# Threshold attention with a feed-forward block: three small moves in the hand-written order of the work

## The chip, the cores and the metric

The kernel runs on one core of a Trainium2 chip. The core has five engines that work side by side: TensorE (PE; its weight loads are shown as PEld), VectorE (DVE), ScalarE (ACT), GpSimd (POOL) and SyncE (SP), which here mostly issues DMA transfers. Each engine takes its instructions strictly in the order in which the program lists them, and waits where an instruction needs something from another engine or from a transfer. The metric is the time of one execution in microseconds (us), less is better. Before the change it is 1319.89 us, the median of three runs (1319.29 to 1322.22).

## What is computed

Eight batches, eight heads, 576 tokens, head width 64; everything is float32, apart from the two weight matrices, which arrive as float64.

```python
scores = scale * np.matmul(q, k.transpose(0, 1, 3, 2))
thresh = np.max(scores, axis=-1, keepdims=True) - tau
scores = np.where(scores >= thresh, scores, -1000000000.0)
scores = scores - np.max(scores, axis=-1, keepdims=True)
attn = np.exp(scores)
attn = attn / (np.sum(attn, axis=-1, keepdims=True) + 1e-09)
attn_out = np.matmul(attn, v)
...
mu = np.mean(x, axis=-1, keepdims=True)          # x: attn_out, heads side by side, width 512
var = np.mean((x - mu) ** 2, axis=-1, keepdims=True)
xn = (x - mu) / np.sqrt(var + 1e-06) * g_ln
ch = np.maximum(xn @ w_ch1, 0.0) @ w_ch2          # 512 -> 2048 -> 512
out = x + ch
```

## The kernel before, in words

**Slots.** The attention is cut into 72 slots, nine for each batch (`SLOTS`). In a slot TensorE makes four 128x576 blocks of scores (`scores`, L434), in two PSUM tiles of two blocks each. VectorE takes the negated maxima of each tile (L450, two reductions), ScalarE exponentials (L463, four), VectorE multiplies them by the mask of the threshold and sums (L473, four), GpSimd divides (L490). VectorE then transposes the blocks in 32x32 pieces (L559), SP writes them to a scratch tensor in DRAM (`scr`, L580) and reads them back in another arrangement (`em`, L594, and `er`, L599); TensorE multiplies them by the values (L638, and L649 for the last 64 tokens) near the end of the next slot, and ScalarE copies the result to x (L663). The scratch write and the read back therefore have most of a slot (some 17 us) for themselves.

**Loads of q and k.** A unit is a pair of heads; its q and k lie in one buffer each (`q_in`, `k_in`). `turn` (VectorE, L368 to L378, after GpSimd's scaling of q at L350) transposes them into the operands of the scores; only then may `load_qk` (eight DMA issues, L120) fetch the next unit's. From slot 11 on, the loads that belong to the first three slots of a batch are put off to the place called "behind", which is after the scratch write of that slot (18 loads in all). The load in a batch's last slot stands right behind `turn`, ahead of the scratch write.

**Groups.** The feed-forward part works on 16 groups of 288 tokens (`g`), two for each batch, and its matmuls are dealt out between those of the slots. When the x of a group is complete, `group_ready` lays out: the mean over features as a matmul (L710, spread by ScalarE, L718), the difference x minus mean (`centre`, L744: four operations of 128x288 on VectorE, one for each block of features, into `xc`), the squares (L1463, ScalarE; added by GpSimd, L1032), and `sum_x` (L946): three differences of blocks of `xc` on VectorE and a fourth on GpSimd, which the matmuls "chain" and "sc<-t" read. `xc` feeds the first matmuls directly. For even groups centring and the three differences stand ahead of the slot's maxima in VectorE's order, with one addition (L1224) of the group before behind them; for odd groups they end just before the next slot. `sum_early` draws such additions forward.

**PSUM for the feed-forward matmuls** is one pool of two banks (`ps_ff`). A new product must wait until ScalarE has copied the one before the last out of its bank: the copies `last`, `part` and `y` (L1199), of a chain (L978), of a hidden tile (L1071).

**Weights.** float64 is turned into float32 on the chip, in 32 pieces (`Weights`): two ScalarE operations (L277, L282), three on VectorE (`begin`, L292 to L299), one or two on GpSimd (`carry`, L307 and L310). This happens within the first eleven slots. A table `BEGUN` says how many pieces each part of a slot begins; `carry_all` then issues GpSimd's part of all pieces that were begun, newest first. In the slots from the sixth on it stands behind the maxima, GpSimd's thresholds (L454) and the first two exponentials. The raw pieces are fetched by SP into whatever buffer is free (`stage`, `x_room`, `y_room` and others).

**Sums of weights.** `sums_of_w1` (L910: three small operations on VectorE and one on GpSimd each time) is advanced at every twelfth step of the second half of groups 1 and 2.

The order on each engine is the order of the calls in the main loop (L1513 on); `at_quarter` puts a call at a place of a slot ("-3", 0, "behind" and so on), and `run` issues what was put there.

Of the kernel before, what the change touches and what calls it, by code (L numbers as in the profile page):

```python
# [12 lines left out]
ALU = mybir.AluOpType  # L13
# [5 lines left out]
def kernel(  # L19
# [37 lines left out]
    NK = DM // 128  # L57
# [3 lines left out]
    TOK = S // 2  # L61
    QH = 256
    SLOTS = 2 * HP + 1
# [31 lines left out]
    units = [(b, hp) for b in range(B) for hp in range(HP)]  # L95
# [33 lines left out]
    def load_v(u):  # L129
# [21 lines left out]
        out=tau_sb, in_=bass.AP(tensor=tau.tensor, offset=tau.offset, ap=[[0, 128], [1, 1]])  # L151
# [5 lines left out]
    for t in v_rest:  # L157
# [9 lines left out]
        out=scl_sb, in0=tau_sb, scalar1=0.0, scalar2=SCALE, op0=ALU.is_ge, op1=ALU.mult  # L167
    )
    nc.vector.tensor_scalar(
        out=low_sb, in0=tau_sb, scalar1=0.0, scalar2=BIG, op0=ALU.is_lt, op1=ALU.mult  # L170
    )
    nc.vector.scalar_tensor_tensor(
        out=low_sb, in0=tau_sb, scalar=-1.0, in1=low_sb, op0=ALU.mult, op1=ALU.subtract
# [5 lines left out]
    class Weights:  # L179
# [141 lines left out]
        def carry_all(self):  # L321

            self.prepare_to(0, False)
            for i in reversed(range(self.carried, self.begun)):
                self.carry(i)
            self.carried = self.begun

# [19 lines left out]
    def scale_q(u, q_in):  # L347

        for at in (slice(0, 8), slice(8, NB)) if u == 0 else (slice(0, NB),):
            nc.gpsimd.tensor_scalar(  # L350
                out=q_in[:, at], in0=q_in[:, at], scalar1=scl_sb, scalar2=1.0,
                op0=ALU.mult, op1=ALU.mult,
            )
# [251 lines left out]
    groups, sums = {}, {}  # L605
# [129 lines left out]
    def centre(g):  # L735
        nonlocal issued
        while waiting_mean:
            issued += next(queue[0])[1]
        xc = centred[g] = ffn.tile([128, NK, TOK], F32, tag="xc", bufs=1, name="xc")
        mean = means.pop(g)  # L740
        while any(d[4] in EARLY for d in drops):
            drops.pop(0)[-1]()
        for c in range(NK):
            nc.vector.tensor_tensor(  # L744
                out=xc[:, c], in0=groups[g][:, c], in1=mean, op=ALU.subtract
            )


# [607 lines left out]
    def ffn_steps(g):  # L1356
        if g in carried:
            yield from carried.pop(g)
        rb = yield from (first_part if g < 2 else first_units)(g)
        sums = sums_of_w1({1: (0, 1), 2: (2,)}.get(g, ()))  # L1360
        for i, step in enumerate((second_quarters if g else second_plain)(g, rb)):
            if i % 12 == 11:
                next(sums, None)
            yield step

# [19 lines left out]
    def at_quarter(n, i, fn, *args):  # L1385
        later_calls.setdefault((n, i), []).append((fn, args))

    def run(n, i):
        for fn, args in later_calls.pop((n, i), ()):
            fn(*args)  # L1390
# [58 lines left out]
    def group_ready(g):  # L1449
        first = divmod(ready(g), QUARTERS)  # L1450
        before = divmod(ready(g) - 1, QUARTERS) if g else first
        if g == 1:
            at_quarter(*before, lambda: among.append(g))
        else:
            at_quarter(*before, mean_of, g)
            at_quarter(*(first if g and first[1] else before), centre, g)
            if g > 1:
                sq = squares_of(g)
                at_quarter(*before, sum_x, g, (0, 1, 2))
                at_quarter(first[0], -3, sum_early, *(("12",) if g == 2 else EARLY))  # L1460
                at_quarter(
                    first[0], -3,
                    lambda: nc.scalar.activation(sq, centred[g], func=AF.Square),  # L1463
                )
                at_quarter(first[0], -1, add_squares, sq, 1, 2)
                at_quarter(first[0], 1, add_squares, sq, 3)
                at_quarter(first[0], 1, sum_x, g, (3,))
        at_quarter(*first, lambda: queue.append(ffn_steps(g)))
# [44 lines left out]
    for n in range(NS):  # L1513
        b, s = divmod(n, SLOTS)
        masks_at, behind_at, end_at = BEGUN[min(n, len(BEGUN) - 1)]
        run(n, -3)
        if n == 1:
            constants(26)
        scores(b, s)
        run(n, -2)  # L1520
        run(n, -1)
        if n + 1 < HP:
            scale_q(n + 1, loaded[n + 1][0])
        rest = exponentials(n)
        es, thr = next(rest)
        conversion.carry_all()
        run(n, 0)
        if n == HP + 2:
            next(rest, None)
        if n >= HP:  # L1530
            conversion.fetch(1 if n == FIRST + 2 else 3, -1 if n > FIRST else 1)
        run_first(stores)
        if early_at(n):
            convert(masks_at)
        second_part(n, 0)
        while drops and drops[0][0] is nc.gpsimd:
            drops.pop(0)[-1]()
        next(rest, None)

        run(n, "load")  # L1540
        if n >= SLOTS - 2 and (n + 2) % SLOTS < HP and n < NS - 2:
            at_quarter(n, "behind", load_v, (n + 2) // SLOTS * HP + (n + 2) % SLOTS)
        u = (n + 1) // SLOTS * HP + (n + 1) % SLOTS
        if (n + 1) % SLOTS < HP and u < len(units):
            turn(u)
            if n > SLOTS + 1 and n % SLOTS < SLOTS - 1 and u + 1 < len(units):
                at_quarter(n, "behind", load_qk, u + 1)
            elif u + 1 < len(units) and u != 2:
                load_qk(u + 1 if u > 1 else 3)
        if n < HP:  # L1550
            conversion.fetch(2 if n else 1)
        if n < SLOTS + HP:
            run_all(aside)
        if not early_at(n):
            convert(masks_at)
        if n < FIRST:
            conversion.prepare_to(end_at)
        elif n == FIRST:
            conversion.prepare_to(behind_at, False)
        run(n, 1)  # L1560
        second_part(n, 1)
        if n > FIRST:
            conversion.prepare_to(behind_at, False)
        blocks_go = by_blocks(n)
        diags = weights(n, es, thr, blocks_go)
        run_all(aside)
        drip()
        if n < SLOTS:
            run_all(stores)
        conversion.begin_to(behind_at)  # L1570
        run(n, 2)
        second_part(n, 2)
        if n < FIRST:
            conversion.carry_all()
        box = []
        if blocks_go:
            conversion.fetch(0 if n == FIRST + 2 else 3, wait=0)
            conversion.prepare_to(end_at, False)
            scr = turn_blocks(b, s, es)
            for fn, args in reversed(later_calls.pop((n, "behind"), ())):  # L1580
                fn(*args)
            run_all(sums_due)
            if n == FIRST:
                conversion.take(e_room[1])
            if n == FIRST:
                conversion.fetch(3)
            conversion.carry_all()
            at_quarter(n + 1, 0, lambda b=b, s=s, scr=scr, box=box: box.append(fetch(b, s, scr)))
        else:

            made = turn_weights(s, es, diags)
            for i, at in enumerate(
                (-1, -1, 0, 0)
            ):
                if i == 3 and n + 1 == FIRST:
                    at_quarter(n + 1, 0, conversion.prepare_to, BEGUN[n + 1][0], False)
                if i < 3:
                    at_quarter(n + 1, at, next, made)
                else:
                    at_quarter(n + 1, at, lambda made=made, box=box: box.append(next(made)))  # L1600
        at_quarter(
            n + 1, 1 if b == 0 and s <= HP else 3,
            lambda b=b, s=s, box=box: values_of(b, s, box[0]),
        )
        if s in (HP, 2 * HP):
            group_ready(2 * b + (s > HP))
        if not plain_at(n):
            run_all(aside)
        drip({nc.vector: 4, nc.gpsimd: 6})
        if HP <= n < FIRST:  # L1610
            conversion.fetch(5)
        run(n, 3)
        if b == 0 and s < HP - 1:
            load_v(s + 1)
        if n < FIRST:
            conversion.prepare_to(BEGUN[n + 1][0] - (n == FIRST - 1))
        second_part(n, 3)
        conversion.begin_to(end_at)
        if n < FIRST:
            conversion.carry_all()  # L1620
        conversion.prepare_to(0, False)
        if FIRST <= n < SLOTS:
            conversion.prepare_to(BEGUN[n + 1][0], False)
        if not plain_at(n):
            run_all(aside)
        drip({nc.vector: 2, nc.gpsimd: 0})
# [40 lines left out]
```

## Time and profile before

| | before |
|---|---|
| median of 3 runs | 1319.89 us |
| the profiled execution | 1319.15 us |
| its span, first to last instruction | 1317.3 us |
| mean granted TensorE clock | 0.995 |
| busy: PE, PEld | 1272.3, 1081.5 us |
| busy: DVE, POOL, ACT | 953.4, 677.1, 528.1 us |

The profile is of one execution. A row of the timeline reads: start in us, duration in us, engine, line of the kernel, operation, output<-input and its shape, how many instructions were merged into the row, and in brackets the idle time of the engine before it with what ended it. A row of the view of waits reads: who, at which line, waited for whom; total in us, how often, the longest. TensorE's fp32 matmul appears as two records, so "x16" is four calls of `product`. Durations of merged rows run from the start of the first to the end of the last. Busy times overlap between engines, so they don't add up to the span.

### The profile page before, as it was taken

The numbers are of one execution on the slowest core, as the hardware profiler recorded it, in microseconds if no ns is written. First come the engines' busy times: TensorE is split into PE (matmuls) and PEld (weight loads), VectorE is DVE, ScalarE is ACT, GpSimd is POOL, SyncE is SP. The second block draws the span as 40 slices with busy tenths as digits, with TensorE's granted clock in tenths as the row PEclk, the third lists the DMA queues.
The fourth block names the chain that finished last, engine by engine and source line by source line (L and its number), as shares of the span: only waits on it lengthen the run. The fifth ranks groups of instructions, "written<-read, shape, count | busy, mean of one in ns | idle before, by whom it ended". The sixth has DMA issues, their size and how long they took to land.

```text
span 1317.3 us, 44852 instructions
## 1 busy us (share of the span) xinstructions
PE 1272.3 (97%) x19272; PEld 1081.5 (82%) x19272; DVE 953.4 (72%) x1760; ACT 528.1 (40%) x1189; POOL 677.1 (51%) x888
## 2 busy tenths in 40 slices
PE   8999889999999999999999999999999999999997
PEld 6765556878888898988989898988989889888987
DVE  7879877987778767677867777787676768777122
ACT  5866242242433424343343434334343423434231
POOL 3465565544537364545636454364645456364324
PEclk9999899999999999999999999999999999999999
DMA  8947856565655767466665667547675666554211
GB/s 165 267 130 184 202 161 180 188 186 159 187 188 175 212 158 209 154 196 182 163 196 191 192 166 183 196 155 211 168 208 173 195 170 167 175 187 167 52 44 20
DMA packets 337478, 226.01 MB, mean 172 GB/s; under 512 B 247616, under 2 KB 292928, under 8 KB 329216
## 3 DMA queue, kind: packets, MB, share of 16 engines
q1 hardware_dynamic: 331168, 222.26, 58.3%
q8 instruction: 151, 2.47, 0.8%
q10 hardware_dynamic: 5952, 0.74, 0.4%
q0 software_dynamic: 160, 0.15, 0.1%
q14 instruction: 47, 0.39, 0.1%
HBM read 134.22 MB, written 88.87 MB: 169 GB/s over the span
## 4 chain that ended last, share of the span: by engine, by line
PE 64%; DVE 6%; DMA 4%; POOL 2%; SPq 1%; issue 1%; ACT 1%; POOLq 0%; DVEq 0%; ACTq 0%
PE seg L103 22%; PE chain L103 11%; PE p L103 9%; PE sc L434 7%; PE sc L638 7%; PE sc L103 6%; DVE e L473 2%; DMA er<-scr 2%; PE sc L649 2%; DVE neg L450 1%; DMA scr<-e 1%; SPq L120 1%; DVE e L559 1%; ACT e L463 1%; POOL sum L692 1%
## 5 line engine op out<-in xcount | busy, mean ns | idle before, releaser
L450 DVE TENSOR_REDUCE neg<-sc 128x2 f32<-128x1152 f32 x144 | 188.9, 1353 | 176.4 <-PE sc L434 174.9
L490 POOL TENSOR_SCALAR e<-e,den 128x576 f32<-128x576 f32 x264 | 205.5, 791 | 111.5 <-DVE den L478 111.3
L103 PE MATMUL seg<-hidden,w 128*64 128x144 f32 x3840 | 249.7, 288 | 2.6 <-DVE hidden L1183 2.6
L103 PE MATMUL p<-xc,w 128*64 128x288 f32 (+1 forms) x2128 | 240.3, 371 | 8.9 <-ACT last L1199 7.4
L103 PEld LDWEIGHTS seg<-hidden,w 128*64 128x64 f32 x3840 | 236.4, 138 | 13.2 <-issue 12.3
L473 DVE SCALAR_TENSOR_TENSOR e<-sc,thr,e 128x576 f32<-128x576 f32 x288 | 222.4, 810 | 20.3 <-POOL thr L454 11.5
L103 PEld LDWEIGHTS p<-xc,w 128*64 128x64 f32 x2128 | 142.3, 137 | 81.3 <-ACT last L1199 9.1
L463 ACT ACTIVATE e<-sc,neg 128x576 f32<-128x576 f32 x288 | 193.5, 751 | 8.1 <-DMA scr<-e 4.9
L454 POOL TENSOR_SCALAR thr<-neg,low_sb 128x2 f32<-128x2 f32 x144 | 39.5, 275 | 303.4 <-DVE neg L450 300.0
L559 DVE STREAM_TRANSPOSE e<-e 128x1152 f32<-128x1152 f32 (+1 forms) x113 | 163.7, 1451 | 24.8 <-POOL e L490 24.5
L1183 POOL TENSOR_TENSOR hidden<-hidden 128x576 f32<-128x576 f32 x86 | 120.2, 1427 | 55.2 <-ACT hidden L1018 52.4
L434 PE MATMUL sc<-kT,qT 64*64 64x384 f32 (+3 forms) x2048 | 140.3, 403 | 3.1 <-DVE e L473 2.1
L638 PE MATMUL sc<-em,v_in 128*64 128x128 f32 (+1 forms) x2368 | 131.5, 265 | 5.3 <-DMA em<-scr 2.6
L638 PEld LDWEIGHTS sc<-em,v_in 128*64 128x64 f32 x2368 | 123.2, 138 | 8.7 <-DVE e L473 3.2
L103 PE MATMUL seg<-hidden,stage 128*64 128x144 f32 x1920 | 124.3, 287 | 0.0
L103 PEld LDWEIGHTS seg<-hidden,stage 128*64 128x64 f32 x1920 | 117.0, 137 | 4.8 <-issue 4.8
L434 PEld LDWEIGHTS sc<-kT,qT 64*64 64x64 f32 x2048 | 76.3, 133 | 44.6 <-issue 21.4
L103 PE MATMUL chain<-t,extra 128*64 128x144 f32 x1312 | 94.3, 286 | 0.0
L103 PEld LDWEIGHTS chain<-t,extra 128*64 128x64 f32 x1312 | 82.1, 137 | 0.0
L663 ACT COPY x<-sc 128x128 f32<-128x128 f32 x120 | 31.3, 264 | 126.0 <-PE sc L434 64.1
L1032 POOL TENSOR_TENSOR hidden<-hidden 128x288 f32<-128x288 f32 x48 | 40.1, 835 | 56.5 <-ACT hidden L1463 55.0
L1199 ACT COPY part<-seg 128x288 f32<-128x288 f32 x54 | 21.8, 406 | 117.1 <-PE seg L103 95.8
(165 smaller groups left out, 1758.4 us busy)
## 6 DMA issues: line engine op xcount, KB each, us to landing
scr<-e SPq DMA_DIRECT2D x60, 1152.0 KB, 4.9
em<-scr SPq DMA_DIRECT2D x63, 1024.0 KB, 5.9
extra<-sums SPq DMA_DIRECT2D x13, 768.0 KB, 5.8
out_dram<-ot SPq DMA_DIRECT2D x248, 36.0 KB, 4.1
q_in<-in_q_dram SPq DMA_DIRECT2D x120, 72.0 KB, 4.6
er<-scr SPq DMA_DIRECT2D x132, 64.0 KB, 5.5
k_in<-in_k_dram SPq DMA_DIRECT2D x116, 72.0 KB, 3.3
v_in<-in_v_dram SPq DMA_DIRECT2D x28, 256.0 KB, 5.4
```

What stands on the lines that cost most here:

```text
L103: nc.tensor.matmul(out[r], lhsT=lhsT[:, r], rhs=rhs, **flags)
L434: mm = nc.tensor.matmul(sc[h][64 * i : 64 * i + 64, at : at + n], lhsT=ql[r] if s == HP else qT[r, half, j * 128 + 64 * i : j * 128 + 64 * ...
L450: nc.vector.tensor_reduce(out=neg[:, i], in_=pairs[h], axis=AXL.X, op=ALU.max, negate=True,)
L454: nc.gpsimd.tensor_scalar(out=thr[:, i], in0=neg[:, i], scalar1=-1.0, scalar2=low_sb, op0=ALU.mult, op1=ALU.add,)
L463: nc.scalar.activation(blocks_of(es, i, n), like(blocks[i], n), func=AF.Exp, bias=neg[:, i : i + 1])
L473: nc.vector.scalar_tensor_tensor(out=e, in0=like(blocks[i], n), scalar=thr[:, i : i + 1], in1=e, op0=ALU.is_ge, op1=ALU.mult, accum_out=de ...
L490: nc.gpsimd.tensor_scalar(out=e, in0=e, scalar1=den[:, i : i + 1], scalar2=1.0, op0=ALU.mult, op1=ALU.mult,)
L559: nc.vector.transpose(et[:, :, at], et[:, :, at])
L638: mm = nc.tensor.matmul(dst[64 * h : 64 * h + 64], lhsT=vt[:, h, c, :], rhs=pick(em[:, 2 * j : 2 * j + 2, c], h), start=c == 0 and first, ...
L663: nc.scalar.copy(x_of(2 * b + (s > HP))[:, s % (HP + 1), 128 * j : 128 * j + 128], pv[j])
L1032: nc.gpsimd.tensor_tensor(out=sq[:, 0], in0=sq[:, 0], in1=sq[:, c], op=ALU.add)
L1183: eng.tensor_tensor(out=out[at], in0=in0[at], in1=in1[at], op=op)
```

## The change

There are four edits in the diff.

1. For even groups the three differences of `sum_x` move behind the maxima (place 0 of the slot instead of the place before it), and the call of `sum_early` goes for them. From group 3 on, centring is one operation of 128x1152 with the mean broadcast over the four blocks.
2. `carry_all` takes the pieces oldest first, and its call moves from behind the first half of `exponentials` to ahead of it, so GpSimd's part of a piece stands ahead of the thresholds. As a consequence one piece is fetched into `y_room` instead of `stage`.
3. The sums of the weights are advanced at every tenth step instead of every twelfth.
4. All loads of q and k stand right behind `turn`, ahead of the scratch write; the load of v stays behind it.

TensorE's order is the same, instruction for instruction. On VectorE the three differences of groups 2, 4, ... 14 stand behind two maxima, thirteen centrings become one operation each, and the sums of weights stand earlier by a few places in five slots. On GpSimd the order of `carry` changes in slots 6 to 10; in group 2 two operations of `finish` (L1236, L1224, of 128x576) move ahead of the fourth difference and of the divisions (L490). On SP the eight issues of q and k change places with the scratch write in 18 slots. ScalarE's order is the same.

```diff
         def carry_all(self):
             self.prepare_to(0, False)
-            for i in reversed(range(self.carried, self.begun)):
+            for i in range(self.carried, self.begun):
                 self.carry(i)
...
-        for c in range(NK):
+        step = NK if g > 2 else 1
+        for c in range(0, NK, step):
             nc.vector.tensor_tensor(
-                out=xc[:, c], in0=groups[g][:, c], in1=mean, op=ALU.subtract
+                out=xc[:, c : c + step], in0=groups[g][:, c : c + step],
+                in1=mean.unsqueeze(1).to_broadcast([128, step, TOK]), op=ALU.subtract,
             )
...
-            if i % 12 == 11:
+            if i % 10 == 9:
                 next(sums, None)
...
                 sq = squares_of(g)
-                at_quarter(*before, sum_x, g, (0, 1, 2))
-                at_quarter(first[0], -3, sum_early, *(("12",) if g == 2 else EARLY))
+                if g % 2:
+                    at_quarter(*before, sum_x, g, (0, 1, 2))
+                    at_quarter(first[0], -3, sum_early, *EARLY)
+                else:
+                    at_quarter(first[0], 0, sum_x, g, (0, 1, 2))
...
+        conversion.carry_all()
         rest = exponentials(n)
         es, thr = next(rest)
-        conversion.carry_all()
         run(n, 0)
...
             turn(u)
-            if n > SLOTS + 1 and n % SLOTS < SLOTS - 1 and u + 1 < len(units):
-                at_quarter(n, "behind", load_qk, u + 1)
-            elif u + 1 < len(units) and u != 2:
+            if u + 1 < len(units) and u != 2:
                 load_qk(u + 1 if u > 1 else 3)
...
             scr = turn_blocks(b, s, es)
-            for fn, args in reversed(later_calls.pop((n, "behind"), ())):
-                fn(*args)
+            run(n, "behind")
```

## The prediction, made before the change was run

> **What bounds the kernel now.** First the head of the page, then the view of waits of TensorE.
>
> ```profile
> span 1317.3 us, 44852 instructions
> ...
> PE 1272.3 (97%) x19272; PEld 1081.5 (82%) x19272; DVE 953.4 (72%) x1760; ACT 528.1 (40%) x1189; POOL 677.1 (51%) x888
> ```
>
> ```profile
> PE p L103 <- ACT last L1199: 7.4, 6, 1.8
> PE p L103 <- POOL w L307: 7.1, 4, 4.1
> PE seg L103 <- DVE hidden L1183: 2.6, 1, 2.6
> PE sc L638 <- DMA em<-scr: 2.6, 2, 1.7
> ```
>
> TensorE is busy 97% of the span, and its instructions and their order do not change. So the time can fall only where TensorE now waits (1317.3 - 1272.3 = 45 us, part of it start and tail), or runs slowly just behind a wait, and rise only where a new wait appears. The four rows are waits that the edits touch, 19.7 us together.
>
> **Edit 1, even groups.** Rows picked from the timeline of group 8, around 723 us; groups 4 to 14 look alike.
>
> ```profile
> 722.85 2.12 PE L434 MATMUL sc<-kT,qT 64*64 64x384 f32 x32
> 723.49 1.56 DVE L744 TENSOR_TENSOR xc<-x,sum 128x288 f32<-128x288 f32 x4
> 725.45 0.46 DVE L946 TENSOR_TENSOR t<-xc,t 128x288 f32<-128x288 f32 x1
> 726.56 2.62 DVE L450 TENSOR_REDUCE neg<-sc 128x2 f32<-128x1152 f32 x2
> 728.11 2.64 ACT L463 ACTIVATE e<-sc,neg 128x576 f32<-128x576 f32 x4
> 728.87 1.15 PE L103 MATMUL chain<-xc,w 128*64 128x144 f32 x16
> 729.58 0.82 DVE L473 SCALAR_TENSOR_TENSOR e<-sc,thr,e 128x576 f32<-128x576 f32 x1 [0.40 <-POOL thr L454]
> 730.61 0.43 ACT L1199 COPY last<-seg 128x288 f32<-128x288 f32 x1
> 731.09 1.20 PE L103 MATMUL p<-xc,w 128*64 128x144 f32 x16 [1.07 <-ACT last L1199]
> 732.12 1.15 PE L103 MATMUL chain<-t,extra 128*64 128x144 f32 x16
> ```
>
> The scores end at 722.85 + 2.12 = 724.97, but the maxima start at 726.56, since three differences and an addition (about 0.46 each) stand ahead of them. The exponentials follow the maxima, and ScalarE's copy `last`, which frees the bank for `p`, stands behind all four: TensorE waits 1.07 us. With the differences behind, the maxima start at about 725.0, 1.6 us earlier; the exponentials end at about 729.2, the copy at about 729.7, and that is before the chain ends (728.87 + 1.15 = 730.02). The wait goes. What is late next: the second difference, which the chain at 732.12 - 1.07 = 731.05 reads. It ends at 725.0 + 2.62 + 2 x 0.46 = 728.5, 2.5 us early. The masks (L473) start after 725.0 + 2.62 + 4 x 0.46 = 729.4, as now (729.58), so the transposes and the scratch write keep their time. Six groups: 7.4 us, of which I leave 0.2 where centring is later than here. **-7.2 us**.
>
> Centring as one operation: its four took 1.56. One of 1152 should cost no more; with the broadcast I have these neighbours on GpSimd, multiplication by a broadcast operand and an addition without one:
>
> ```profile
> 273.47 1.42 POOL L1236 TENSOR_TENSOR y<-y,rb 128x576 f32<-128x576 f32 x1
> 274.97 1.41 POOL L1224 TENSOR_TENSOR y<-y,x 128x576 f32<-128x576 f32 x1
> ```
>
> A broadcast costs nothing there. I take 1.3 us, bounds 1.2 and 3.1 (half the rate). At 3.1 the maxima would start when they do now, and the 7.2 us would be lost, not more; in odd groups VectorE waits for the scores afterwards, which hides it.
>
> Group 2 is apart, with a like wait behind two exponentials:
>
> ```profile
> 268.77 1.20 PE L103 MATMUL chain<-xc,w 128*64 128x144 f32 x16 [1.52 <-ACT hidden L1071]
> ```
>
> Some 1.2 us of it should go. But there the two GpSimd operations above (2.83 us) now stand ahead of the divisions, so the transposes and the additions that free the scores' banks come later, by about 0.6 us too late for the next scores. **-0.6 us** (0 to -1.5).
>
> **Edit 4, q and k ahead of the write.** Slots 18 and 19, from VectorE's timeline, and TensorE's with a stretch of equal size before:
>
> ```profile
> 302.13 0.20 DVE L378 STREAM_TRANSPOSE q_last<-q_in 128x64 f32<-128x64 f32 x1
> 316.29 2.62 DVE L450 TENSOR_REDUCE neg<-sc 128x2 f32<-128x1152 f32 x2 [1.76 <-PE sc L434]
> 323.52 0.78 DVE L368 STREAM_TRANSPOSE kT<-k_in 128x576 f32<-128x576 f32 x1 [3.76 <-DMA k_in<-in_k_dram]
> 329.15 1.41 DVE L1183 TENSOR_TENSOR hidden<-hidden 128x576 f32<-128x576 f32 x2
> ```
>
> ```profile
> 231.66 2.43 PE L103 MATMUL seg<-hidden,w 128*64 128x144 f32 x36
> 330.04 4.10 PE L103 MATMUL seg<-hidden,w 128*64 128x144 f32 x36 [2.61 <-DVE hidden L1183]
> ```
>
> The buffers are free at 302.3, yet the loads are issued only behind the scratch write, which waits for the transposes of that slot; VectorE then waits 3.76 us for k, everything behind it is late, and TensorE waits 2.61 us for L1183, and runs the 36 records behind it in 4.10 us instead of 2.43. Loaded from 302.3 on, k is there by 315 even if issuing takes the 6.3 us of the SP rows below and landing the 5.9 us of a read (page row below), before the maxima end at 318.9. L1183 then ends some 3.7 us earlier and TensorE doesn't wait: 2.61 + 1.67 = 4.28. **-4.3 us**. [...]
>
> The same eight issues stand between write and read of slot 11, whose values are the longer of the two waits for `em` (1.7 in the waits above):
>
> ```profile
> 198.97 0.35 SPq L580 DMA_DIRECT2D scr<-extra  x1
> 199.42 3.51 SPq L120 DMA_DIRECT2D q_in<-in_q_dram  x4
> 205.77 0.57 SPq L594 DMA_DIRECT2D em<-scr  x1
> ```
>
> Write to read is 6.8 us. A batch's last slot already loads ahead of the write; there it is 5.1 us, and the write is not late:
>
> ```profile
> 748.20 1.97 SPq L120 DMA_DIRECT2D q_in<-in_q_dram  x4
> 754.44 0.36 SPq L580 DMA_DIRECT2D scr<-e  x1
> 759.58 0.38 SPq L594 DMA_DIRECT2D em<-scr  x1
> ```
>
> So the read comes 1.7 us earlier. **-1.7 us** (0 to -1.7). In all later slots TensorE doesn't wait for `em`, so nothing is gained or lost there.
>
> **Edit 2, pieces in order and first.** VectorE, ScalarE and TensorE in slots 9 and 10:
>
> ```profile
> 146.27 0.77 DVE L372 STREAM_TRANSPOSE qT<-q_in 128x256 f32<-128x256 f32 x2 [2.97 <-POOL q_in L350]
> ...
> 163.78 2.62 DVE L450 TENSOR_REDUCE neg<-sc 128x2 f32<-128x1152 f32 x2 [2.01 <-PE sc L434]
> ```
>
> ```profile
> 154.49 0.68 ACT L277 ACTIVATE w<-x_room 128x512 f32<-128x512 f32 x1 [8.92 <-DMA x_room<-in_moe_w_ch_dram]
> ```
>
> ```profile
> 145.56 4.10 PE L103 MATMUL p<-hidden,w 128*64 128x288 f32 x32 [1.23 <-POOL w L307]
> 153.74 3.15 PE L103 MATMUL p<-hidden,w 128*64 128x288 f32 x12 [4.08 <-POOL w L307]
> ```
>
> GpSimd does two pieces just before 145.5, behind the thresholds and newest first; TensorE waits for the second (1.23), and VectorE 2.97 us for the scaled q behind them. Both pieces were ready before the maxima, so ahead of the thresholds they cost nothing: the 1.23 go, and VectorE gains some 2.4 us. The next pair comes that much earlier and in the right order, and most of the 4.08 goes. But not all of this is gain: piece 29 is bound by its load, which lands at 154.49 whatever happens, so the pieces behind it, up to the last, gain only what VectorE loses now between 155 and 167: the 2.01 us wait for the scores and about 0.9 us of faster operations. TensorE then waits elsewhere for 29 to 31. I take **-2.5 us**; bounds 0 (the load binds everything) and -8.7 (the four waits, 7.1, and 1.6 for the 12 records that took 3.15 us behind the longest: at the rate of the 32 above them, 4.10, they take 1.54).
>
> **Edit 3** moves three operations of 0.3 us ahead of maxima for which VectorE waits anyway (1.76 us at 316.29): 0. `y_room` for `stage`: another address, 0.
>
> **Sum:** -7.2 - 0.6 - 4.3 - 1.7 - 2.5 = -16.3. The profiled execution took 1319.15, so 1302.9; the median of the three runs lies 0.74 above it, so 1303.6, about **1303.5 us**.
>
> **Rivals.** (a) The early gains are swallowed: before 220 us VectorE and the loads hand the lead to and fro, and 1.7 + 2.5 come back as other waits for `em` or the last pieces. Then -12.1: 1307.8. For it: the wait of 8.92 us for a load. Against: SP's order relieves that stretch too.
>
> (b) Only part of the even groups or of the wait at 330 us goes (a broadcast at half rate, or another copy that is late): about -7, 1313.
>
> (c) The other side: the write comes late. In the 18 slots the write now stands behind eight issues and their packets. The SP rows of slot 11 show eight issues taking 205.77 - 199.42 = 6.3 us, and these rows show the room:
>
> ```profile
> 765.25 0.20 DVE L378 STREAM_TRANSPOSE q_last<-q_in 128x64 f32<-128x64 f32 x1
> ...
> 770.93 1.92 PE L638 MATMUL sc<-em,v_in 128*64 128x128 f32 x32
> 771.76 0.35 SPq L580 DMA_DIRECT2D scr<-e  x1
> ```
>
> The read issued at 759.58 lands after a median of 5.9 us (page row below), at 765.5, and is needed at 770.93: 5.4 us of room.
>
> ```profile
> em<-scr SPq DMA_DIRECT2D x63, 1024.0 KB, 5.9
> ```
>
> Issues from 765.45 on that take 6.3 us end at 771.8, just when the write is ready; TensorE is hurt only if issues and packets make the write more than 5.4 us late. From there each microsecond costs 18: at 7.0 us late, 29 us against the 16.3, 1332. Against it stands the batch's last slot, 754.44, with no delay at all. [...]
>
> (d) The change does nothing: each wait is replaced by the next: 1317 to 1322.
>
> **How the numbers follow.** Forecast 0.62, (a) 0.17, (b) 0.10, (c) 0.06, (d) 0.05. The range takes in forecast, (a), most of (b), and a conversion that gains 3 us more than I take: 1299 to 1313. A measurement of this kernel can tell about 0.2%, 2.6 us, from no change: faster 0.89, within 0.04, slower 0.07.
>
> **What would show it.** In the changed kernel's waits of TensorE the row for `last` L1199 should be gone or under 1 us; that for L1183 gone, and the 36 records behind it at 2.4 us; that for L307 not over 5 us; no new row for `em` past 230 us. The write should still be issued as soon as the transposes end. Wrong would be: `p` waiting as before (then the copy is held by something else than the exponentials), a chain waiting for a difference, or `em` waits that repeat in every batch.

## The result and the profile after

The changed kernel takes 1307.13 us, the median of four runs (1306.81 to 1307.69); the kernel before, run beside it, took 1321.06 us (1319.29 to 1322.31). The ratio is 0.9896, with a 95% interval of 0.9879 to 0.9913: 14 us faster. The profiled execution took 1306.81 us, 12.3 us less than that of before, where 16.3 us were forecast.

The head of the page of the changed kernel: TensorE's work is as it was, and the span is 12.3 us shorter.

```profile
span 1305.0 us, 44839 instructions
...
PE 1270.6 (97%) x19272; PEld 1081.2 (83%) x19272; DVE 962.3 (74%) x1721; ACT 529.2 (41%) x1189; POOL 681.3 (52%) x888
```

VectorE has 39 instructions fewer (13 centrings of one operation for four) and is yet 8.9 us longer busy. That is the first sign that something runs slower. The view of TensorE's waits (total, times, longest):

```profile
PE sc L638 <- DMA em<-scr: 4.6, 3, 2.3
PE sc L638 <- DVE e L473: 3.7, 3, 1.3
PE p L103 <- POOL w L307: 2.9, 2, 2.3
```

and of the same view, for the stretch from 230 us to the end alone:

```profile
PE sc L103 <- DVE e L473: 1.4, 6, 0.5
PE sc L434 <- DVE hidden L986: 0.2, 1, 0.2
PE p L103 <- ACT last L1201: 0.2, 1, 0.2
```

The wait for `last`, 7.4 us before, is 0.2 us, and the wait for L1183 (now L1185) has no row. The wait for `em`, 2.6 us before, is 4.6 us, all of it ahead of 230 us; beside it the mask (L473) has a row three times as long as before (1.3 us there).

**Where the time went**, slot by slot. This table is worked out from the timelines of VectorE: the start of a slot's first maxima (L450) in the kernel before, and for every other kernel of this study how much later (+) or earlier (-) the same instruction starts in its profiled execution. A column that steps down by 1.6 us between two rows has gained 1.6 us between them. Each column is one execution. The names of the columns are explained with the experiments.

```
before us | changed | newest,ahead | newest,behind | oldest,behind | hybrid | sums at 12 | sums x alone | qk alone | x and qk | x and 10
   72.46  |  +0.1   |    0.0       |    +0.2       |     0.0       |   0.0  |    0.0     |    +0.5      |   0.0    |   +0.3   |   +0.1
  117.50  |  +5.5   |   +0.1       |    +0.1       |    +6.0       |  -0.4  |   -0.2     |    +0.9      |  +0.6    |   +0.1   |   +0.3
  140.00  |  +7.7   |   +0.1       |    +0.1       |    +7.2       |  -0.4  |   -0.2     |    +0.9      |  +0.6    |   +0.1   |   +0.3
  200.78  |  +4.1   |   -2.3       |    -1.1       |    +6.2       |  -3.0  |   -3.4     |    -0.2      |  +0.3    |   -1.0   |   +0.1
  218.03  |  +2.6   |   -3.9       |    -1.7       |    +4.3       |  -4.2  |   -4.9     |    +2.7      |  -0.9    |   -2.3   |   +0.1
  247.23  |  +2.6   |   -3.9       |    -1.7       |    +4.3       |  -4.1  |   -4.9     |    +2.7      |  -0.9    |   -2.3   |   +0.1
  265.49  |  -0.6   |   -6.9       |    -4.7       |    +1.3       |  -7.2  |   -6.3     |    +1.2      |  -0.9    |   -4.4   |   -2.9
  297.68  |  +0.7   |   -5.7       |    -3.5       |    +2.6       |  -6.0  |   -2.6     |    +4.9      |  -0.9    |   -2.4   |   -1.7
  357.96  |  -4.4   |  -10.7       |    -8.2       |    -2.5       | -10.8  |   -7.1     |    +4.9      |  -5.7    |   -7.2   |   +0.2
  403.85  |  -4.4   |  -10.7       |    -8.2       |    -2.4       | -10.8  |   -7.1     |    +4.9      |  -5.4    |   -7.2   |   +0.3
  743.48  |  -8.9   |  -14.9       |   -12.6       |    -6.9       | -15.3  |  -11.5     |    +0.6      |  -5.6    |  -11.4   |   -4.0
span      | 1305.0  |  1298.9      |  1301.5       |  1306.8       | 1298.9 |  1302.3    |   1314.0     | 1312.0   |  1302.4  | 1309.8
```

From 200 us on the changed kernel gains what was forecast, and a little more: at 1201.97 us, the last slot, it is 12.7 us ahead. But up to 140 us it has lost 7.7 us, and 4.1 us of them are still missing at 200 us.

**An even group.** Group 8 again, from the timelines of VectorE, ScalarE and TensorE:

```profile
717.41 2.62 DVE L450 TENSOR_REDUCE neg<-sc 128x2 f32<-128x1152 f32 x2 [0.16 <-PE sc L434]
719.95 0.57 DVE L948 TENSOR_TENSOR t<-xc 128x288 f32<-128x288 f32 x1
```

```profile
721.50 0.41 ACT L1201 COPY last<-seg 128x288 f32<-128x288 f32 x1
```

```profile
721.28 1.15 PE L103 MATMUL chain<-xc,w 128*64 128x144 f32 x16
722.26 1.15 PE L103 MATMUL p<-xc,w 128*64 128x144 f32 x16
723.24 1.15 PE L103 MATMUL chain<-t,extra 128*64 128x144 f32 x16
```

The maxima now wait for the scores, 0.16 us, where before three differences stood in front of them; the copy `last` ends at 721.91 us, before the chain does (722.43), and `p` follows without a bracket. The chain that reads the differences doesn't wait for them.

**q and k ahead of the write.** SP's queue, VectorE and TensorE around the slot that lost 4.3 us before. The first two rows belong to the slot ahead of it, the next three to the slot itself:

```profile
306.81 2.63 SPq L120 DMA_DIRECT2D k_in<-in_k_dram  x4
313.93 0.36 SPq L580 DMA_DIRECT2D scr<-e  x1
...
324.93 2.78 SPq L120 DMA_DIRECT2D q_in<-in_q_dram  x4
327.75 3.85 SPq L120 DMA_DIRECT2D k_in<-in_k_dram  x4
331.70 0.57 SPq L580 DMA_DIRECT2D scr<-e  x1
```

```profile
320.80 0.77 DVE L368 STREAM_TRANSPOSE kT<-k_in 128x576 f32<-128x576 f32 x1
```

```profile
324.01 6.29 PE L103 MATMUL seg<-hidden,w 128*64 128x144 f32 x100
```

The load of k is issued ahead of the write, and VectorE, which waited 3.76 us for k before, takes it up without a bracket. The matmuls of `seg` now run through, 0.06 us each, where 36 records took 4.10 us behind the wait.

**The stretch that lost time**, 80 to 118 us, first VectorE and GpSimd, then VectorE's transposes for the scratch write, then TensorE:

```profile
80.88 0.42 DVE L292 TENSOR_SCALAR w<-w 128x512 f32<-128x512 f32 x1
81.33 1.40 DVE L295 TENSOR_SCALAR w<-w 128x512 uint32<-128x512 uint32 x1
82.77 1.06 DVE L299 SCALAR_TENSOR_TENSOR w<-extra,w 128x512 uint32<-128x512 uint32 x1
...
96.83 2.62 DVE L569 STREAM_TRANSPOSE extra<-e 128x1152 f32<-128x1152 f32 x2
```

```profile
81.10 1.35 POOL L307 TENSOR_TENSOR w<-w,extra 128x512 int32<-128x512 int32 x1 [5.34 <-issue]
82.56 0.74 POOL L310 TENSOR_SCALAR w<-w,g_sb 128x512 f32<-128x512 f32 x1
```

```profile
113.87 0.44 PE L638 MATMUL sc<-em,v_in 128*64 128x128 f32 x4 [2.31 <-DMA em<-scr]
115.78 2.38 PE L638 MATMUL sc<-em,v_in 128*64 128x128 f32 x28 [1.48 <-DMA em<-scr]
```

The same stretch before, VectorE and GpSimd:

```profile
81.22 0.43 DVE L295 TENSOR_SCALAR w<-w 128x512 uint32<-128x512 uint32 x1
...
86.19 0.80 DVE L295 TENSOR_SCALAR w<-w 128x512 uint32<-128x512 uint32 x1
...
92.70 2.62 DVE L569 STREAM_TRANSPOSE extra<-e 128x1152 f32<-128x1152 f32 x2
```

```profile
86.70 4.59 POOL L490 TENSOR_SCALAR e<-e,den 128x576 f32<-128x576 f32 x4
```

There L295 takes 0.43 us with nothing of GpSimd's beside it, and 0.80 us beside L310 and the divisions. In the changed kernel GpSimd begins the older piece at 81.10 us, as soon as VectorE has left it, while VectorE is still at the next one. VectorE's L295, started 0.23 us later, takes 1.40 us and ends 0.28 us behind GpSimd's operation; L299 takes 1.06 us beside L310. Newest first, GpSimd's first operation needs VectorE's last one, so that this overlap did not occur. In the changed kernel it comes again at the later lists of pieces: six more operations of L295, between 106 and 157 us, took 1.38 to 1.40 us. The transposes start at 96.83 us (92.70 before), `em` is read back 4.1 us later, and TensorE waits 2.31 and 1.48 us for it.

### The profile page after: what moved, and what is told of

The parts are those of the page before. It is cut to its first block, busy times and chain, and to the rows that moved or that the text cites. A ratio compares the mean times of both kernels' runs of the same rounds, so it can differ in the third digit from the quotient of the medians.

```text
span 1305.0 us, 44839 instructions
## 1 busy us (share of the span) xinstructions
PE 1270.6 (97%) x19272; PEld 1081.2 (83%) x19272; DVE 962.3 (74%) x1721; ACT 529.2 (41%) x1189; POOL 681.3 (52%) x888
## 4 chain that ended last, share of the span: by engine, by line
PE 76%; DVE 7%; POOL 3%; issue 2%; DMA 1%; SPq 1%; ACT 1%; POOLq 0%; DVEq 0%; ACTq 0%
PE seg L103 28%; PE p L103 11%; PE chain L103 11%; PE sc L434 9%; PE sc L638 8%; PE sc L103 6%; PE sc L649 2%; DVE neg L450 2%; DVE e L473 1%; POOL q_in L350 1%; POOL sum L692 1%; SPq L120 1%; DVE extra L569 1%; DVE qT L372 1%; POOL e L490 1%
## 5 line engine op out<-in xcount | busy, mean ns | idle before, releaser
L450 DVE TENSOR_REDUCE neg<-sc 128x2 f32<-128x1152 f32 x144 | 188.8, 1352 | 166.0 <-PE sc L434 164.8
L490 POOL TENSOR_SCALAR e<-e,den 128x576 f32<-128x576 f32 x264 | 203.0, 781 | 110.3 <-DVE den L478 110.2
L473 DVE SCALAR_TENSOR_TENSOR e<-sc,thr,e 128x576 f32<-128x576 f32 x288 | 222.1, 808 | 16.6 <-POOL thr L454 8.0
L454 POOL TENSOR_SCALAR thr<-neg,low_sb 128x2 f32<-128x2 f32 x144 | 44.1, 308 | 284.6 <-DVE neg L450 283.5
L1185 POOL TENSOR_TENSOR hidden<-hidden 128x576 f32<-128x576 f32 x86 | 119.6, 1419 | 52.5 <-ACT hidden L1020 52.5
L986 DVE TENSOR_TENSOR hidden<-sc,hidden 128x288 f32<-128x288 f32 x123 | 52.4, 454 | 21.3 <-PE sc L103 13.8
```

Source lines behind the costliest of these rows:

```text
L450: nc.vector.tensor_reduce(out=neg[:, i], in_=pairs[h], axis=AXL.X, op=ALU.max, negate=True,)
L454: nc.gpsimd.tensor_scalar(out=thr[:, i], in0=neg[:, i], scalar1=-1.0, scalar2=low_sb, op0=ALU.mult, op1=ALU.add,)
L473: nc.vector.scalar_tensor_tensor(out=e, in0=like(blocks[i], n), scalar=thr[:, i : i + 1], in1=e, op0=ALU.is_ge, op1=ALU.mult, accum_out=de ...
L490: nc.gpsimd.tensor_scalar(out=e, in0=e, scalar1=den[:, i : i + 1], scalar2=1.0, op0=ALU.mult, op1=ALU.mult,)
L986: ins = nc.vector.tensor_tensor(out=out, in0=a, in1=b, op=ALU.add)
L1185: eng.tensor_tensor(out=out[at], in0=in0[at], in1=in1[at], op=op)
```

## The experiments

**Theory A**: oldest first is what costs, because GpSimd's share of a piece then runs beside VectorE's share of the next, and VectorE is what the scratch write waits for. **Theory B**: the place costs, since pieces ahead of the thresholds keep GpSimd from them. Four kernels take edit 2 apart; all else is as in the changed kernel. They ran on one chip, beside before at 1322.05 us.

**1. Newest first, ahead** (column "newest,ahead").

```diff
-            for i in range(self.carried, self.begun):
+            for i in reversed(range(self.carried, self.begun)):
```

> The changed kernel (1307.1 us) with carry_all going through the new pieces newest first again; the call stays ahead of the exponentials, and the other edits stay. Theory A (beside each other): oldest first, GpSimd's L307/L310 start on a piece that VectorE has left while VectorE is still at L292/L295/L299 of the next ones, and both slow down; at the scores of slot 8 that has cost 7.2 us, of which 3.8 us are left from 182 us on. It expects 1303.3 us (1307.1 - 3.8; bounds 1300 to 1305), the pieces' VectorE operations at 79 to 94 us short again (0.42 to 1.17 us), the transposes L569 that start at 96.83 us back at about 92.7 us, and the waits for em of 2.31 us and 1.48 us near 114 us gone. Theory B (place): the loss is that the pieces now stand ahead of the thresholds (L454) in GpSimd's queue. It expects no gain: 1307 us or, since GpSimd then waits for VectorE's last piece before the thresholds too, up to 1310 us.

Measured: 1300.36 us (1299.95 to 1300.72), ratio 0.9837 (0.9822 to 0.9851), span 1298.9 us. The rows of the same stretch:

```profile
81.27 0.43 DVE L295 TENSOR_SCALAR w<-w 128x512 uint32<-128x512 uint32 x1
81.73 0.69 DVE L299 SCALAR_TENSOR_TENSOR w<-extra,w 128x512 uint32<-128x512 uint32 x1
...
92.75 2.63 DVE L569 STREAM_TRANSPOSE extra<-e 128x1152 f32<-128x1152 f32 x2
```

```profile
82.56 1.30 POOL L307 TENSOR_TENSOR w<-w,extra 128x512 int32<-128x512 int32 x1 [6.87 <-ACT hidden L1114]
```

L295 is back at 0.43 us, the transposes at 92.75 us. GpSimd starts 0.14 us after VectorE's L299 has ended (81.73 + 0.69 = 82.42); its bracket names a ScalarE operation. Of the waits for `em` at 114 us the longer is gone and one of 1.29 us stays, as theory A had not said; the kernel before has a wait of 1.25 us at that place too. The gain is 6.1 us by the spans, more than the 3.8 us expected, since the kernel also gains 2.3 us on the one before between 140 and 201 us. Theory B falls.

**2. Oldest first, behind** (column "oldest,behind").

```diff
-        conversion.carry_all()
         rest = exponentials(n)
         es, thr = next(rest)
+        conversion.carry_all()
```

> The changed kernel with the call of carry_all back behind the first half of the exponentials and the thresholds; the order stays oldest first. Theory A (beside each other): the overlap of GpSimd's L307/L310 with VectorE's L292 to L299 stays where several pieces follow one another, so 1307 us (bounds 1305 to 1310). Theory B (place ahead of the thresholds): the loss goes, 1303.3 us.

Measured: 1308.65 us (1307.72 to 1309.02), ratio 0.9898 (0.9884 to 0.9913). The loss up to 140 us is there (+7.2), whatever the place.

**3. Edit 2 undone** (column "newest,behind"): both diffs above at once.

> The changed kernel with the edit of the pieces undone in both halves: newest first, behind the first half of the exponentials; the other three edits stay. Both theories put the loss into this edit and expect 1303.3 us (1307.1 - 3.8, the offset that the scores show from 182 us on; bounds 1300 to 1305). The rival to both, that the early loss comes from one of the other edits (the sums of W1 at every 10th step, or q and k ahead of the write), expects 1307 us or more, with the scores of slot 8 at 142 us as before it.

Measured: 1302.81 us (1301.82 to 1306.45), ratio 0.9861 (0.9837 to 0.9884), span 1301.5 us. The loss is in edit 2 and in nothing else. The four kernels make a square, by the spans: ahead instead of behind gains 2.6 us newest first (1301.5 to 1298.9) and 1.8 us oldest first; oldest instead of newest first costs 6.1 us ahead and 5.3 us behind. By the medians the gains are 2.4 and 1.5 us, the costs 6.8 and 5.8 us. What the place is worth is therefore small against the noise (the intervals of experiments 1 and 3 overlap); what the order costs is not.

How VectorE's operation changes shows best in the rows that group L295 between 75 and 260 us: in all these kernels 21 operations of one shape (busy us, mean ns). Before, changed, newest first ahead, and oldest first behind:

```profile
L295 DVE TENSOR_SCALAR w<-w 128x512 uint32<-128x512 uint32 x21 | 12.1, 574 | 0.7
```

```profile
L295 DVE TENSOR_SCALAR w<-w 128x512 uint32<-128x512 uint32 x21 | 18.4, 875 | 0.7
```

```profile
L295 DVE TENSOR_SCALAR w<-w 128x512 uint32<-128x512 uint32 x21 | 11.7, 559 | 0.7
```

```profile
L295 DVE TENSOR_SCALAR w<-w 128x512 uint32<-128x512 uint32 x21 | 17.8, 846 | 0.7
```

The order sets the mean, the place doesn't. In the changed kernel seven of the 21 took 1.38 to 1.40 us, each of them beside an L307 of GpSimd; before and newest first ahead none took more than 0.91 us.

**4. The newest first, then the rest from the oldest on.**

```diff
-            for i in range(self.carried, self.begun):
+            new = list(range(self.carried, self.begun))
+            for i in new[-1:] + new[:-1]:
```

> The changed kernel with one step changed: of the new pieces GpSimd takes the newest first and then the rest from the oldest on, still ahead of the exponentials. GpSimd's first operation then waits for VectorE's last one on the pieces, and little stands beside it; the rest stays in order. Theory A (beside each other) expects the gain of the kernel with the whole list turned round: 1303.3 us (1300 to 1305), VectorE's operations on the pieces at 79 to 94 us short. A rival that takes the order itself (which piece is ready when, which room comes free first) and not the overlap for the cause expects that two thirds and more of the list in order keep the loss: 1306 to 1307 us.

Measured: 1301.75 us (1300.94 to 1302.25), ratio 0.9847 (0.9832 to 0.9861). One piece at the head of the list, the one that VectorE finishes last, brings most of the gain: it isn't the sequence that costs but the moment at which GpSimd may begin. Theory A stands.

**5. Newest first, in order from 150 us on** (column "hybrid"). With the whole list newest first TensorE waits 4.13 us for the older piece of a pair near 150 us. This kernel takes that pair in order. It ran beside before at 1320.35 us, as did 6 to 8.

```diff
-            for i in range(self.carried, self.begun):
+            new = range(self.carried, self.begun)
+            for i in new if self.begun > 27 else reversed(new):
```

> The changed kernel with the new pieces newest first while at most 27 have been begun, and oldest first from there on (one list of two pieces near 150 us is then in order). With the whole list newest first (median 1300.4 us, span 1298.9 us) TensorE waits 4.13 us for the older of those two, which GpSimd takes 1.24 us behind the newer, and only once VectorE is through with both. Theory A (the overlap with VectorE costs where VectorE is on the path, and order pays where TensorE waits for the older piece) expects TensorE to go on 1.2 to 2.9 us earlier at that place: 1298.5 us (1297.4 to 1300). The rival, that the time saved there is swallowed by later waits or that any overlap costs more than order gives, expects 1300.4 us or more.

Measured: 1301.19 us (1300.64 to 1302.77), ratio 0.986 (0.9846 to 0.9874): no gain. TensorE's timeline, first with the whole list newest first, then here:

```profile
152.31 3.15 PE L103 MATMUL p<-hidden,w 128*64 128x288 f32 x12 [4.13 <-POOL w L307]
168.62 2.16 PE L103 MATMUL p<-hidden,w 128*64 128x288 f32 x16 [1.41 <-POOL w L307]
```

```profile
149.12 1.68 PE L103 MATMUL p<-hidden,w 128*64 128x288 f32 x12 [1.09 <-POOL w L307]
...
163.02 1.68 PE L103 MATMUL p<-hidden,w 128*64 128x288 f32 x12 [1.17 <-POOL w L307]
167.99 2.16 PE L103 MATMUL p<-hidden,w 128*64 128x288 f32 x16 [2.56 <-POOL w L307]
```

TensorE goes on 3.2 us earlier and then waits for the next pieces: at the third row only 0.6 us of the 3.2 are left, and at the end of the table's 300 us 0.3.

**6. The differences of even groups moved, alone** (column "sums x alone"): before, with the change of `sum_x` of edit 1 and nothing else.

> The kernel before with one thing of the change: the differences of the even groups (and group 2's share of them) behind the maxima; centring stays four operations, the pieces, the sums of W1, q and k stay as before. The prediction's terms for it were -7.2 us (even groups) and -0.6 us (group 2): span 1309.5 us where that of before is 1317.3 us, ratio 0.994. By the offsets of the scores in the changed kernel's trace (about 8.3 us from the even groups behind 388 us and 0.9 us from group 2) it is a little more: span 1308 us, ratio 0.993. The rival in which part of it is swallowed (1313 us on record) expects half: span 1313 us, ratio 0.997.

Measured: 1315.17 us (1312.96 to 1317.14), ratio 0.9963 (0.995 to 0.9976), by the ratio 4.9 us; the span is 1314.0 us. That is near the rival's number, but not by its mechanism: from 404 us on, each even group gains its 1.3 to 1.6 us. What is missing is lost at two places ahead of that. TensorE's timeline:

```profile
212.75 2.81 PE L638 MATMUL sc<-em,v_in 128*64 128x128 f32 x32 [2.86 <-DMA em<-scr]
...
280.24 0.47 PE L710 MATMUL var<-hidden,avg_sb 128*64 128x144 f32 x4 [0.87 <-DVE hidden L984]
...
281.75 3.86 PE L434 MATMUL sc<-kT,qT 64*64 64x384 f32 x32 [0.67 <-DVE hidden L984]
```

The wait for `em` at 212 us was 1.66 us before, and this kernel changes nothing ahead of it; experiment 9, with the same order there, has 1.67 us, so this part is not the edit's. The one at 280 us belongs to the edit, and experiments 9 to 11 are about it.

**7. q and k ahead of the write, alone** (column "qk alone"): before with edit 4 and nothing else.

> The kernel before with one thing of the change: q and k are loaded ahead of the write in slots 11 to 16 instead of behind it. The prediction's terms were -4.3 us (the wait at 330 us) and -1.7 us (em of slot 11): span 1311.3 us, ratio 0.9955. By the offsets in the changed kernel's trace (-4.5 us at 330 us, -1.3 us at 216 us) span 1311.5 us. The rival on record in which q and k make the write and em late expects 1332 us; the rival that only the wait at 330 us goes expects span 1313 us, ratio 0.9966.

Measured: 1313.37 us (1312.07 to 1316.46), ratio 0.9951 (0.9939 to 0.9963), span 1312.0 us: 5.3 us by the spans, where 6.0 us were forecast (the edit moves the loads in all 18 slots, not in slots 11 to 16 alone): slot 11 gains 1.2 us, the stretch from 298 to 358 us 4.8 us.

**8. Centring as four operations again**, in the changed kernel:

```diff
-        step = NK if g > 2 else 1
+        step = 1
```

> The changed kernel with centring as four operations of 128x288 again. One operation of 128x1152 takes 1.35 us and the four together 1.56 us (both traces), beside TensorE at work. The prediction's term was 0, so 1307.1 us (bounds 1306 to 1308). The rival, that the 0.2 us of each of 13 groups lie on the path because they stand ahead of the maxima, expects up to 1309.5 us.

Measured: 1307.98 us (1307.58 to 1309.63), ratio 0.991 (0.9897 to 0.9923), against 0.9896 (0.9879 to 0.9913). The intervals overlap. By the spans it is 0.9 us, of which 0.4 us are there at 218 us, ahead of the first centring that differs; from 404 us to the end both kernels gain 8.3 us.

The kernels of experiments 6 and 7 gain 11.4 us together by their ratios, and edit 2 undone leaves 18.4 us. **Theory C**: the sums of W1 at every tenth step (edit 3), forecast at 0, are what lets edit 1 pay in group 2. **Theory D**: they do nothing. Three kernels, beside before at 1321.08 us.

**9. Differences moved, and the sums at every tenth step** (column "x and 10"): the kernel of experiment 6 with

```diff
-            if i % 12 == 11:
+            if i % 10 == 9:
```

> The kernel before with two things of the change: the differences of the even groups behind the maxima, and the sums of W1 at every 10th step; q and k stay behind the write. The first alone gave a span of 1314.0 us. Theory C (the waits near 280 us, with slow matmuls some 3.7 us, come from the last W1 sums on VectorE): span 1310 to 1311.5 us, the two waits for the additions near 280 us gone, the wait for em at 213 us still there. Theory D: 1314 us.

Measured: 1311.26 us (1308.16 to 1312.22), ratio 0.9922 (0.991 to 0.9935), span 1309.8 us. Between 247 and 298 us it gains 1.8 us where experiment 6 loses 2.2. Later, with q and k behind the write, it loses 3.3 us between 340 and 358 us, behind a VectorE that waits 3.25 us for k.

**10. Newest first, ahead, with the sums at every twelfth step** (column "sums at 12"): the kernel of experiment 1 with the lines above turned round.

> The kernel with the pieces newest first and ahead (span 1298.9 us) and one more thing undone: the sums of W1 at every 12th step again instead of every 10th. The prediction gave this edit 0. Theory C: the last list of these sums (two additions of 0.7 us and more on VectorE) stands at 256 to 258 us in the kernel before, just ahead of group 2's centring; once the differences of group 2 have been moved behind the maxima the same time is on the path, and the step of 10 takes it away. It expects 2 to 4 us of loss: span 1301 to 1303 us, and TensorE waits for the additions of the first unit (the hidden that VectorE makes, line 986) near 275 us with slow matmuls behind. Theory D (the term of 0 was right): span 1298.9 us within 1 us.

Measured: 1304.01 us (1302.15 to 1304.86), ratio 0.9868 (0.9852 to 0.9883), span 1302.3 us against 1298.9. VectorE and TensorE here:

```profile
252.74 0.72 DVE L912 TENSOR_TENSOR extra<-w 128x128 f32<-128x128 f32 x1
...
269.61 2.82 DVE L559 STREAM_TRANSPOSE e<-e 128x1152 f32<-128x1152 f32 x2 [2.45 <-POOL e L490]
```

```profile
272.83 0.47 PE L710 MATMUL var<-hidden,avg_sb 128*64 128x144 f32 x4 [0.91 <-DVE hidden L986]
274.34 3.61 PE L434 MATMUL sc<-kT,qT 64*64 64x384 f32 x32 [0.67 <-DVE hidden L986]
```

and at the place of the last row, with the sums at every tenth step:

```profile
272.89 2.17 PE L434 MATMUL sc<-kT,qT 64*64 64x384 f32 x32 [0.21 <-DVE hidden L986]
```

With twelve steps the last list of the sums (251.65 to 253.46 us, 1.8 us of VectorE) stands just ahead of group 2's centring; with ten it has been done by 248 us. Everything behind it on VectorE and, over the divisions (L490), on GpSimd is late by that much, up to the additions for which the next scores wait. Theory C stands, theory D falls.

**11. Differences moved, and q and k ahead** (column "x and qk"): the kernel of experiment 6 with edit 4.

> The kernel before with two things of the change: the differences of the even groups behind the maxima, and q and k ahead of the write; the W1 sums stay at every 12th step, the pieces newest first and behind, centring four operations. By themselves the two gave spans of 1314.0 us (-3.3) and 1312.0 us (-5.3) against 1317.3 us. If they only add up: span 1308.7 us. Theory C (alone, the first brings new waits: em at 212.75 us, 2.86 us, which q and k ahead take away, and the additions near 280 us, which only the W1 sums at every 10th step take away): span 1304 to 1307 us. Theory D (q and k are enough for both, the W1 sums do nothing): span 1301.5 us, that of the changed kernel with the pieces as before.

Measured: 1306.48 us (1304.23 to 1307.47), ratio 0.9887 (0.9873 to 0.99), by the ratio 14.9 us; the profiled execution, with a span of 1302.4 us, is the fastest of the four. That span lies nearer to theory D's. The median speaks for theory C: 1306.48 us is 3.7 us more than experiment 3 took, which differs by edit 3 and the merged centring, though the intervals overlap. So the run doesn't decide alone. Taken over all kernels, the three that have the differences moved and the sums at every twelfth step (experiments 6, 10 and 11) show two waits for the additions of some 0.9 and 0.67 us between 272 and 282 us; the eight with ten steps have no wait above 0.6 us there. The two edits gain more together (14.9 us) than one by one (4.9 and 6.5), by a margin little wider than the three intervals allow for.

## Why the prediction was right, and which step failed

The direction and the size held: 1307.13 us against 1303.5. By the table, the forecast of 16.3 us missed what the last slot shows, 12.7 us, by 3.6 us: one step 6.6 us too good, the others 3.0 us too cautious. That the total came this near is in part luck, since errors of opposite sign made up for each other.

- **Even groups, -7.2**: the six groups gave 1.6, 1.6, 1.3, 1.3, 1.3 and 1.3 us, 8.3 us between 404 us and the end. The mechanism is the one forecast, row for row: maxima at the end of the scores, `last` before the end of the chain, differences not waited for. The term was 1.1 us too small.
- **Centring, 0**: one operation takes 1.35 us where four took 1.56 (in group 3 alone it took 1.93); 1.3 had been taken, and the half rate is excluded. Experiment 8 finds no gain in the steady groups.
- **Group 2, -0.6, and edit 3, 0**: together the changed kernel gains 1.9 us between 247 and 298 us: 3.2 us up to 265 us, of which 1.3 us are lost again behind it. The forecast had both signs (1.2 and 0.6 us). But the split between the two edits was wrong. Without edit 3 the same place costs 2.3 us (experiment 10) or 2.2 us (experiment 6); with it, it gains 1.8 us (experiments 1 and 9). Edit 3 is worth about 4 us there, 3.4 us of the span. In the profiled execution of experiment 11 it is less: without edit 3 the stretch still gains 0.1 us. Its 0 rested on the row at 316 us, one of the five slots in which the sums move, where VectorE waits for scores; near 255 us VectorE doesn't wait, and the step that moved the differences had just put VectorE on the path.
- **q and k, -4.3 and -1.7**: the wait for L1183 is gone and the records behind it are fast, 0.06 us each where 36 took 4.10 us; 5.1 us between 298 and 358 us and 1.5 us in slot 11. Alone it is worth 5.3 us of the span. The other side, a write that comes late by more than its room, did not occur. In the slot shown above the transposes end at 330.38 us and the write is issued at 331.70 us, 1.3 us late behind the eight issues. So the sign "as soon as the transposes end" failed in three of the 18 slots, with writes 0.7, 1.3 and 1.4 us late (at 203.8, 331.7 and 348.7 us). This is well inside the 5.4 us of room: behind 230 us TensorE never waits for `em`.
- **Edit 2, -2.5: the step that failed.** It measured as a loss: the changed kernel is 4.1 us late at 200 us, and without edit 2 it is faster by 3.5 us of the span (4.3 us by the medians). The step had two halves, and only the half on the place was right: ahead instead of behind gains 2.6 us by the spans (experiments 1 and 3). That this is nearly the number of the whole term is in part luck. The wait of 1.23 us near 145 us goes as forecast, but the next one, of which "most" was to go, is 4.13 us in experiment 1 and was 4.08, and about half of the 2.6 us comes only behind 200 us. The half "in the right order" took as free that GpSimd starts on a piece early; and where order alone was tried on that later pair (experiment 5), the time gained came back as other waits. The bounds, 0 and -8.7, left no room for a loss, and a loss could have been looked for: the kernel before has rows in which VectorE's operations on pieces stand beside GpSimd's divisions and take longer (L295 at 86.19 us, 0.80 us, shown above), and the step never asked which operations the new order would set side by side. The number of rival (a), 1307.8, is nearer to the result than the forecast, and waits for `em` did take its place; but its cause, gains handed back, is not what happened: undoing the order alone gives 1300.4.

What the overlap does is in the rows of the changed kernel: L295 (0.43 us alone), begun 0.23 us behind L307, took 1.40 us and ended 0.28 us behind L307's end, and L299 (0.69 us alone) took 1.06 us beside L310. The runs show that the overlap costs, and how much: oldest instead of newest first, 6.1 us of the span ahead and 5.3 us behind. By what means one engine slows the other they do not show.

**Open**: why 32 records of scores behind waits of 0.91 and 0.67 us took 3.61 us in experiment 10, and 2.17 us behind waits of 0.89 and 0.67 us in experiment 11 (3.86 us in experiment 6, behind 0.87 and 0.67). The profile's windows, from 274.3 us in experiment 10 and from 276.1 us in experiment 11, give a mean granted clock (the column after POOL's) of 0.58 and 1.00:

```profile
274.30:278.00 3.70, 3.66 (x34) 1.82 (x36) 1.49 (x5) 3.32 (x9) 0.00 (x0) 0.58 0.98 292
```

```profile
276.10:280.00 3.90, 3.85 (x46) 2.18 (x48) 2.96 (x6) 3.77 (x12) 0.17 (x1) 1.00 0.93 277
```

What decides is not settled by these runs, and 1.4 us of what edit 3 is worth hangs on it.

The best version found is that of experiment 1: the change with the pieces newest first again, 1300.36 us, ratio 0.9837 (0.9822 to 0.9851).

## What to carry to other kernels

Before letting a second engine start earlier, list what the first engine does at that moment: here 6.1 us of the span went (1305.0 us oldest first, 1298.9 us newest first) because GpSimd no longer waited for VectorE to be through, though no instruction was added. An order that looks backwards may hold two engines apart, and undoing half of it (one piece at the head of the list) shows that cheaply. And when an edit takes a wait away, ask of the other edits which of them makes room for what is late next: an edit forecast at 0 from the old schedule was worth 3.4 us in the new one (alone in the old one it was not run).

## What the runs showed of the hardware that was not expected

A VectorE operation on 128x512 words (L295) took 0.43 us by itself and, in the changed kernel, up to 1.40 us beside a GpSimd addition of 1.35 us; over 21 of them the mean went from 559 ns (experiment 1) to 875 ns (changed). The granted clock was 0.58 in the mean over the 3.7 us after waits of 0.91 and 0.67 us (experiment 10; 1.6 us of waiting within 2.4 us); in experiment 11, with waits of 0.89 and 0.67 us, it was 1.00 over 3.9 us.
